# A gated-recurrence and feed-forward kernel: the last token tile's second layer in two column parts, and room for the factor DMAs in SyncE's queue

## The chip, the cores and the metric

The kernel runs on one core of one Trainium2 chip. The metric is the device time of one execution in microseconds, as the median of several timed runs. Beside them stands one profiled execution, from which all durations below are taken. Engines are named TensorE (PE in the profile), VectorE (DVE), ScalarE (ACT), GpSimd (POOL) and SyncE (SP).

## The reference

Two steps follow each other. For each of 4 batches and 8 heads, a state of 48 x 48 runs over 768 time steps:

```python
for t in range(S):
    state = alpha[:, :, t, :, None] * state + np.einsum('bhd,bhe->bhde', k[:, :, t], v[:, :, t])
    y[:, :, t] = np.einsum('bhd,bhde->bhe', q[:, :, t], state)
```

The result, with heads side by side, is x with 3072 tokens of 384 numbers. Then a feed-forward block:

```python
h = x @ w_in            # 384 -> 2048
r = np.maximum(h, 0.0)
g = r * r
return (g @ w_out).astype(np.float32)   # 2048 -> 384
```

Inputs and the output are float32.

## The kernel before

**Tiles.** The 3072 tokens are 24 chunks of 128, six for each batch. One chunk s is also one token tile of the feed-forward block. The recurrence is done in chunk form: ScalarE takes the logarithm of alpha (`L_s`, L404), TensorE sums it along the chunk with a triangular matrix (step p0), ScalarE takes exponentials of that (`A` or `Af`, L432, and `Ainv`, L436), VectorE forms `qA_s` = q x A (L462) and `kI_s` = k x Ainv (L465), TensorE transposes both (steps p1q, p1k, L256), and from there come masked scores (`sm`, L526), the state (`st`) and the chunk's output. The state is multiplied once for each chunk by the chunk's total factor (`ae_s`, L560), and a copy of it (`sb`, L565) serves the next chunk. GpSimd casts v (`vb`, L409).

**Feed-forward.** For each group of token tiles, the first layer's matmuls (`bank<-xT_big,w_in_b`) are followed by a ReLU on ScalarE (`r`, L814) and a square on VectorE (`gT`, L822); the second layer (`bank<-w_out_b,gT`) runs 16 matmuls of 384 columns for each token tile, in four quarters, into one PSUM bank. The tile's result is copied to `ob` (L852 on VectorE or L854 on ScalarE) and stored by a DMA of 192 KB from SyncE's queue (L861; L864 for the first four tiles).

**The factor.** For chunks below `TURN` = 12 the chunk's factor comes out of TensorE and ScalarE. From chunk 12 on it is the last row of `Af`, brought to the partitions of `ae_s` by two small DMAs, also from SyncE's queue (`e_aed`, L447 to L449).

**The order.** The order of all instructions on each engine is worked out before the launch by a planner (class `Plan`). Each operation has an engine, a duration and what it depends on; `run` places the operation that can start first, and at the end `self.order.sort(key=lambda o: o.start)` gives the order in which all are emitted. The planner has columns that are no engine of their own: "DMA" for the loads, first in first out; "OUT" for the stores; "SPD" for the factor DMAs. All three are emitted into the one queue of SyncE, which issues in order and waits where the next DMA has to wait. A placed store pushes the DMA column back by its duration:

```python
            if eng == "OUT":
                free["DMA"] = max(free.get("DMA", 0.0), t) + op.dur
```

A factor DMA does not. A store's `start` is moved back by `OUT_LATE` = 3.5 (attribute `late`, line 865) against the time at which it is ready, so that it is emitted behind what the planner places in these 3.5.

**Loads.** Each chunk has four loads of 192 KB, in the order at (alpha), qt, kt, vt (`add_load`, L347). The buffers hold pairs of chunks, three pairs deep (`LB` = 6 chunks). The planner lets the load of chunk s start when the use of the same tensor of chunk s-6 is done (`prev`), and counts `LD` = 1.05 for it.

**Durations in the planner** that the change meets: a quarter of the second layer 0.65; the copy of a tile on ScalarE 0.38; steps from an operation's end to its users 0.05 behind the second layer, 0.14 behind ScalarE, 0.13 behind VectorE; `Af` 0.76; `qA_s` from chunk 12 on 0.78; a store 0.55; a factor pair 0.4, landing `AE_LAT` = 4.0 later. They set orders only.

Of the kernel before, what the change touches and what calls it, by code (L numbers as in the profile page):

```python
# [8 lines left out]
FP32 = mybir.dt.float32  # L9
# [47 lines left out]
def after(op, x=0.0):  # L57
    return (op, x)


class Plan:
# [37 lines left out]
    def run(self, gate):  # L99
        free = self.free  # L100
        while any(self.pending.values()):
            best = None
            for eng, ops in self.pending.items():
                t0 = free.get(eng, 0.0)
                pick = None
                fifo = eng in ("DMA",)
                for op in (ops[:1] if fifo else ops):
                    if not gate(op):
                        continue
                    r = self.ready(op)  # L110
                    if r is None:
                        continue
                    if len(op.durs) > 1:
                        ends = {e: max(r, free.get(e, 0.0)) + x + LAT[e] for e, x in op.durs.items()}
                        if ends[eng] > min(ends.values()):
                            continue
                    key = (max(r, t0), op.prio)
                    if pick is None or key < pick[0]:
                        pick = (key, op)
                if pick is not None and (best is None or pick[0][0] < best[0]):  # L120
                    best = (pick[0][0], eng, pick[1])
            assert best is not None, "nothing can run"
            t, eng, op = best
            for e in op.durs:
                self.pending[e].remove(op)
            op.eng, op.dur = eng, op.durs[eng]
            op.start = t + getattr(op, "late", 0.0)
            if eng == "DMA" and self.pauses and t >= self.pauses[0][0]:
                op.dur += self.pauses.pop(0)[1]
            free[eng] = t + op.dur  # L130
            if op.lat is None:
                op.lat = LAT.get(eng, 0.2)
            if eng == "OUT":
                free["DMA"] = max(free.get("DMA", 0.0), t) + op.dur
            op.done = t + op.dur + op.lat
            if op.takes is not None:
                self.ready(op)
                op.slot.release.append(op.gives if op.gives is not None else op)
            self.order.append(op)
            self.on_pick(op)  # L140
        self.order.sort(key=lambda o: o.start)
# [3 lines left out]
def kernel(  # L145
# [10 lines left out]
    nc = tc.nc  # L156
    B, H, S, D = q.shape
    HD = H * D
    P = 128
# [3 lines left out]
    d_model, d_ff = moe_w_in.shape  # L163
    n_tok = out.shape[0]
    KT = d_model // P
    FT = d_ff // P
    NT = n_tok // P
# [5 lines left out]
    out_r = out.rearrange("(tt p) n -> tt p n", p=P)  # L173
# [7 lines left out]
    LB = 6  # L181
# [3 lines left out]
    opool = ctx.enter_context(tc.tile_pool(name="opool", bufs=9))  # L185
# [15 lines left out]
        out=utri_f, in_=ones_f, compare_op=ALU.is_ge, fill=0.0,  # L201
# [4 lines left out]
        out=sutri_f, in_=ones_f, compare_op=ALU.is_ge, fill=0.0,  # L206
# [25 lines left out]
    w_out_b = consts.tile([P, FT, d_model], BF16)  # L232

    NBUF = 4
    TURN = 12
# [13 lines left out]
    def pin(ins):  # L249
        tc.keep_in_program_order(ins)  # L250

    def mm(*a, **kw):
        pin(nc.tensor.matmul(*a, **kw))  # L253
# [4 lines left out]
    plan = Plan()  # L258
# [9 lines left out]
    def psum(op, shape, dt):  # L268
        i = op.slot.bank
        return banks[i].tile(shape, dt, name=f"bank{i}")  # L270
    X_SLACK = 0.2
    LD = 1.05
# [4 lines left out]
    def add(eng, dur, emit, *deps, **kw):  # L277
        return plan.add(Op(eng, dur, emit, deps, **kw))
# [42 lines left out]
    def w_dep(which, f):  # L321
        return w_ready[which][[hi > f for hi in W_CUT[which][1:]].index(True)]

    C = [dict() for _ in range(NT)]
# [13 lines left out]
    def add_load(s, nm):  # L338
        d = C[s]
        b, c = divmod(s, NCH)  # L340
        k = s // 2

        def ld():
            if s % 2 == 0:
                PAIR[k][nm] = loads.tile([P, 2, H, D], FP32, name=nm)
            d[nm] = PAIR[k][nm][:, s % 2]
            pin(nc.sync.dma_start(out=d[nm], in_=SRC[nm][b, c]))  # L347
        prev = C[s - LB]["use_" + nm] if s - LB >= 2 * NS else None
        if 2 * NS <= s < 2 * NS + LB and (k - LB // 2) < NS:
            prev = SUP[k - LB // 2]["use_" + nm]  # L350
        d["ld_" + nm] = add("DMA", LD, ld, prev, lat=2.4)

    PAIR = [dict() for _ in range(NT // 2)]
    SRC2 = [("at", alpha), ("qt", q), ("kt", k), ("vt", v)]
# [39 lines left out]
    def add_chunk(s):  # L394
        d = C[s]
# [4 lines left out]
        g = dict(prio=-10.0 + s * 0.01)  # L400
# [49 lines left out]
        if s < TURN:  # L450
            ae0 = add("ACT", 0.18, e_ae0, p0, after(ai), **g)
            p0.gives = ae1 = add("ACT", 0.19, e_ae1, p0, after(ae0), **g)
        else:
            p0.gives = ai
            ae1 = add("SPD", 0.4, e_aed, a_, lat=AE_LAT, **g)

        def e_qA():
            if s < TURN:
                pin(nc.vector.tensor_mul(qA[:, :, 0:D], d["qt"], d["A"]))
            else:  # L460
                v4 = "p (n j) d -> p n j d"
                pin(nc.vector.tensor_mul(qA[:, :, 0:D].rearrange(v4, j=2), d["qt"].rearrange(v4, j=2), d["A"]))  # L462
# [312 lines left out]
    GT = [sum(GN[:i]) for i in range(len(GN))]  # L775
    NG = len(GN)
    gT = {}
    NQ = 4
# [2 lines left out]
    M2_LAST = sl_bank[::-1]  # L781
    OUT_LATE = 3.5
    OUT_AT = 72.0
    RELU_PRIO = -20.0
    RELU_PRIO0 = 0.0
    DUMMY = 1
    COLD = 8.0
    sq = {}
    prog = {"m1": 0.0, "m2": 0.0}

    def add_moe1(g, f0, before, lo=0, hi=None, per=1):
# [20 lines left out]
        def e_relu():  # L812
            box["r"] = rpool.tile([P, 512], BF16, name="r")
            pin(nc.scalar.activation(box["r"][:, 0:w], box["ph"][:, 0:w], AF.Relu))  # L814
        rl = add("ACT", 0.055 + w / 1190.0, e_relu, op, prio=RELU_PRIO if g > 1 else RELU_PRIO0)
        box["first"].gives = rl
# [9 lines left out]
            sq.setdefault((g, f0 + i), []).append(o)  # L826
        return op

    def add_moe2(g, tt, before, box, quarters, pools):

        for qd in quarters:
            def e_mm(qd=qd):
                if qd == 0:
                    box["po"] = psum(box["first"], [P, 512], FP32)[:, 0:d_model]
                for kf in range(qd * FT // NQ, (qd + 1) * FT // NQ):
                    mm(box["po"], lhsT=gT[g][:, kf, tt * P:(tt + 1) * P], rhs=w_out_b[:, kf, :],
                       start=(kf == 0), stop=(kf == FT - 1))
            fs = range(qd * FT // NQ, (qd + 1) * FT // NQ) if g == 0 else range(FT)
            deps = [o for f in fs for o in sq[(g, f)]] + [w_dep("o", fs[-1] if g == 0 else FT - 1)] + ([after(before)] if before else [])
            op = plan.add(Op("PE", 0.65, e_mm, deps, takes=pools if qd == 0 else None, prio=0.1))  # L840
            op.moe = (2, 2.56 / NQ)
            if qd == 0:
                box["first"] = op
            op.lat = 0.05
            before = op
        if quarters[-1] < NQ - 1:
            return op

        def e_ev():
            box["ob"] = opool.tile([P, d_model], FP32, name="ob")  # L850
            if ev.eng == "DVE":
                pin(nc.vector.tensor_copy(box["ob"], box["po"]))  # L852
            else:
                pin(nc.scalar.copy(box["ob"], box["po"]))  # L854
        ev = add({"DVE": 0.47, "ACT": 0.38}, 0, e_ev, op, prio=-15.0)
        box["first"].gives = ev

        def e_out():
            s = GT[g] + tt
            if s >= 2 * NS:  # L860
                pin(nc.sync.dma_start(out=out_r[s], in_=box["ob"]))  # L861
            else:
                for t in range(2):
                    pin(nc.sync.dma_start(out=out2_r[s, t], in_=box["ob"][HF * t:HF * t + HF]))  # L864
        add("OUT", 0.55, e_out, ev, at=OUT_AT + 3.0 * (GT[g] + tt)).late = OUT_LATE
        return op

    DMA_ORDER = ["0 at qt kt vt", "1 at qt kt", "i", "1 vt", "i", "i", "i", "i", "o", "o", "o", "o"]
    for x in DMA_ORDER + [s for s in range(2 * NS, NT) if s not in DMA_ORDER]:
        if x in ("i", "o"):  # L870
            load_w(x)
        elif isinstance(x, str):
            for nm in x[1:].split():
                add_load2(int(x[0]), nm)
            if len(SUP[int(x[0])]) == len(srcs) * 1:
                add_super(int(x[0]))
        else:
            for nm, _ in srcs:
                add_load(x, nm)
            add_chunk(x)  # L880
# [84 lines left out]
```

## Time and profile before

| | |
|---|---|
| median of 3 timed runs | 187.55 us (187.5, 187.55, 188.36) |
| profiled execution | 188.04 us |
| its span | 186.3 us, 5003 instructions |
| busy share of the span: PE, DVE, ACT, POOL | 95%, 73%, 66%, 16% |
| PE matmuls | 1986 |
| DMA moved | 30.23 MB in 100712 packets, mean 162 GB/s |
| stores of a tile (L861) | 20, 192 KB each, 2.5 us median to landing |
| factor DMAs (L449) | 24, 0.8 KB each, 2.0 us median to landing |
| loads (L347) | 20 for each tensor, 192 KB each, 3.7 to 3.8 us median to landing |

The span runs from the first to the last instruction of the profiled execution, and the execution's own time is 1.7 us longer. In the profile's rows the first number is the start in microseconds from the span's start and the second the duration; "x4" counts instructions merged into one row. Rows of SPq are SyncE's issues of DMAs: their duration is that of the issue, with the time it had to wait inside, not that of the transfer. Matmul rows overlap, since the end of a matmul is modelled: the pitch of a run of matmuls is read from their starts.

### The profile page before, as it was taken

To read this page: it belongs to the slowest core of one execution; us is meant where nothing else is said; L and a number is where in the kernel's file an instruction comes from. 1 tells how busy PE (TensorE), PEld (TensorE's weight loads), DVE (VectorE), ACT (ScalarE), POOL (GpSimd) and SP (SyncE) were. 2 spreads that over 40 slices of the span, in tenths; PEclk is the share of its full clock that TensorE was granted. 3 is DMA by queue.
4 is the path that set the end of the run, shared out by engine and by line. 5 is a ranking of instruction groups with operands and counts; after the bars stand their busy time and mean duration, and the time that the engine had idled before them with its cause. 6 is when DMAs were issued, how large, how long until landed. Compare 5 with 4: busy or idle time off the path is not lost.

```text
span 186.3 us, 5003 instructions
## 1 busy us (share of the span) xinstructions
PE 177.9 (95%) x1986; PEld 132.6 (71%) x1987; DVE 136.5 (73%) x281; ACT 122.6 (66%) x257; POOL 29.8 (16%) x47
## 2 busy tenths in 40 slices
PE   7889899999999999999999999799999999999992
PEld 2566684667887877777867878467878778777751
DVE  6688679875996986776997988664997977952500
ACT  3577779457986975847758778428867847744621
POOL 5034777411111121011011012001020000000000
PEclk9999999999999999999999999999999999999999
DMA  6999999799999999892899679888101011011112
GB/s 149 261 279 344 382 372 325 153 219 214 179 183 203 188 197 202 196 205 50 186 250 201 154 173 226 162 184 191 66 0 43 4 44 44 4 42 46 42 48 81
DMA packets 100712, 30.23 MB, mean 162 GB/s; under 512 B 93648, under 2 KB 99536, under 8 KB 100688
## 3 DMA queue, kind: packets, MB, share of 16 engines
q1 hardware_dynamic: 100688, 29.91, 68.4%
q8 instruction: 15, 0.25, 0.6%
q14 instruction: 9, 0.07, 0.1%
HBM read 25.17 MB, written 4.72 MB: 160 GB/s over the span
## 4 chain that ended last, share of the span: by engine, by line
PE 81%; DMA 6%; DVE 4%; ACT 3%; SPq 3%; issue 1%; DVEq 0%; ACTq 0%
PE bank L253 70%; PE bank L256 7%; DMA at<-in_alpha_dram 3%; PE sc L253 2%; SPq L362 2%; PE st L253 2%; DMA vt<-in_v_dram 2%; DMA ae_s<-Af 1%; DVE gT L822 1%; DVE qkT L369 1%; ACT raw L713 1%; ACT r L814 1%; DVE st L560 1%; ACT A L632 0%; ACT L_s L601 0%
## 5 line engine op out<-in xcount | busy, mean ns | idle before, releaser
L253 PE MATMUL bank<-xT_big,w_in_b 128*128 128x256 bf16 (+2 forms) x599 | 73.8, 268 | 0.1
L253 PE MATMUL bank<-w_out_b,gT 128*128 128x384 bf16 x384 | 72.0, 326 | 0.0
L814 ACT ACTIVATE r<-bank 128x512 bf16<-128x512 f32 x96 | 56.6, 602 | 18.3 <-PE bank L253 16.7
L253 PEld LDWEIGHTS <-w_in_b 128*128 128x128 bf16 x600 | 52.9, 98 | 10.0
L822 DVE TENSOR_TENSOR gT<-r 128x512 bf16<-128x512 bf16 x96 | 45.1, 496 | 13.1 <-ACT r L814 12.8
L253 PEld LDWEIGHTS <-gT 128*128 128x128 bf16 x384 | 35.4, 97 | 18.2
L409 POOL CAST vb<-vt 128x384 bf16<-128x384 f32 x20 | 11.3, 566 | 93.8 <-PE bank L253 51.7
L369 DVE COPY qkT<-bank 128x1024 bf16<-128x1024 bf16 (+1 forms) x26 | 16.5, 646 | 2.9 <-PE bank L256 2.7
L854 ACT COPY ob<-bank 128x384 f32<-128x384 f32 x19 | 9.2, 483 | 14.1 <-PE bank L253 14.0
L526 DVE TENSOR_TENSOR sm<-sc,utri_b 128x512 bf16<-128x512 f32 x24 | 15.4, 682 | 2.2 <-PE sc L253 2.2
L367 ACT CAST xn<-bank 128x384 bf16<-128x384 f32 x24 | 11.2, 481 | 8.8 <-PE bank L253 8.6
L369 DVE COPY xT_big<-bank 128x384 bf16<-128x384 bf16 x21 | 7.4, 354 | 10.2 <-PE bank L256 10.1
L253 PEld LDWEIGHTS <-qkT 64*128 64x128 bf16 (+2 forms) x304 | 10.5, 97 | 5.1 <-issue 2.3
L462 DVE TENSOR_TENSOR qA_s<-qt,Af 128x384 bf16<-128x384 f32 x12 | 10.3, 860 | 3.1 <-ACT Af L432 2.9
L565 ACT CAST sb<-st 128x384 bf16<-128x384 f32 x16 | 7.7, 478 | 6.2 <-DVE st L560 6.1
L465 DVE TENSOR_TENSOR kI_s<-kt,Ainv 128x384 bf16<-128x384 f32 x20 | 11.6, 582 | 0.0
L432 ACT ACTIVATE Af<-bank 128x384 f32<-128x384 f32 x12 | 10.4, 865 | 1.2 <-ACT L_s L404 0.6
L256 PE MATMUL bank<-ident_bf,kI_s 128*128 128x128 bf16 x96 | 9.2, 220 | 1.5 <-DVE kI_s L465 1.4
L404 ACT ACTIVATE L_s<-at 128x384 bf16<-128x384 f32 x20 | 10.3, 525 | 0.4 <-DMA at<-in_alpha_dram 0.4
L253 PE MATMUL bank<-warm 128*128 128x256 bf16 (+2 forms) x39 | 8.7, 355 | 1.9 <-DVE both L216 1.1
L560 DVE TENSOR_TENSOR st<-st,ae_s 128x384 f32<-128x384 f32 x16 | 8.9, 558 | 1.9 <-DMA ae_s<-Af 1.8
L436 ACT ACTIVATE Ainv<-bank 128x384 bf16<-128x384 f32 x20 | 10.3, 514 | 0.0
(72 smaller groups left out, 176.7 us busy)
## 6 DMA issues: line engine op xcount, KB each, us to landing
at<-in_alpha_dram SPq DMA_DIRECT2D x20, 192.0 KB, 3.8
qt<-in_q_dram SPq DMA_DIRECT2D x20, 192.0 KB, 3.8
kt<-in_k_dram SPq DMA_DIRECT2D x20, 192.0 KB, 3.7
vt<-in_v_dram SPq DMA_DIRECT2D x20, 192.0 KB, 3.7
out_dram<-ob SPq DMA_DIRECT2D x20, 192.0 KB, 2.5
wo<-in_moe_w_out_dram SPq DMA_DIRECT2D x4, 768.0 KB, 6.9
wi<-in_moe_w_in_dram SPq DMA_DIRECT2D x3, 768.0 KB, 8.0
at<-in_alpha_dram SPq DMA_DIRECT2D x2, 384.0 KB, 4.9
```

Of the source, the lines that this page charges most:

```text
L253: pin(nc.tensor.matmul(*a, **kw))
L256: pin(nc.tensor.transpose(*a))
L367: pin(nc.scalar.copy(out_t, in_t))
L369: pin(nc.vector.tensor_copy(out_t, in_t))
L404: pin(nc.scalar.activation(L[:, :, 0:D], d["at"], AF.Ln))
L409: pin(nc.gpsimd.tensor_copy(d["vb"], d["vt"]))
L432: pin(nc.scalar.activation(d["A"], split(d["pm"][:, 0:HD], s), AF.Exp))
L465: pin(nc.vector.tensor_mul(kI[:, :, 0:D], d["kt"], d["Ai"]))
L526: pin(nc.vector.tensor_mul(d["sm"][:, hh], d["sc"][hh], utri_b.to_broadcast([P, NP, P])))
L560: pin(nc.vector.tensor_mul(st4, st4, bcast(ae, D)))
L814: pin(nc.scalar.activation(box["r"][:, 0:w], box["ph"][:, 0:w], AF.Relu))
L822: pin(nc.vector.tensor_mul(gT[g][:, f0:f0 + per, lo * P:lo * P + n], r, r))
```

## The change

The planner gets three new rules. A factor pair now pushes the DMA column back by 0.5 (`hold`). A load of chunk 14 or later waits in the plan also for the use of the same tensor of chunk s-5 (`pace`). A load of chunk 12 or later counts 0.97 and not 1.05. None of the three adds a wait on the chip by itself; they alter start times in the plan, and so the order of emission.

The last token tile's second layer is computed by a new function, `add_last`: first 16 matmuls for columns 0 to 255 into one bank, then 16 matmuls for columns 256 to 383 into another. Each part has its own copy, always on ScalarE, and its own store, of 128 KB and of 64 KB, without `late`.

```diff
@@ run
+            if hasattr(op, "hold"):
+                free["DMA"] = max(free.get("DMA", 0.0), t) + op.hold
             if eng == "OUT":
                 free["DMA"] = max(free.get("DMA", 0.0), t) + op.dur
@@ add_load
-        d["ld_" + nm] = add("DMA", LD, ld, prev, lat=2.4)
+        pace = C[s - LB + 1]["use_" + nm] if s >= TURN + 2 else None
+        d["ld_" + nm] = add("DMA", LD if s < TURN else 0.97, ld, prev, pace, lat=2.4)
@@ add_chunk
             ae1 = add("SPD", 0.4, e_aed, a_, lat=AE_LAT, **g)
+            ae1.hold = 0.5
@@
+    LAST_COLS = ((0, 256), (256, 384))
@@
+    def add_last(g, tt, before, pools):
+        deps = [o for f in range(FT) for o in sq[(g, f)]] + [w_dep("o", FT - 1)]
+        rows = out_r[GT[g] + tt]
+        for lo, hi in LAST_COLS:
+            box = {}
+            for qd in range(NQ):
+                def e_mm(qd=qd, lo=lo, hi=hi, box=box):
+                    if qd == 0:
+                        box["po"] = psum(box["first"], [P, 512], FP32)[:, 0:hi - lo]
+                    for kf in range(qd * FT // NQ, (qd + 1) * FT // NQ):
+                        mm(box["po"], lhsT=gT[g][:, kf, tt * P:(tt + 1) * P], rhs=w_out_b[:, kf, lo:hi],
+                           start=(kf == 0), stop=(kf == FT - 1))
+                t = 0.65 * (hi - lo) / d_model
+                op = plan.add(Op("PE", t, e_mm, deps + [after(before)], takes=pools if qd == 0 else None, prio=0.1))
+                op.moe = (2, t)
+                box.setdefault("first", op)
+                op.lat = 0.05
+                before = op
+
+            def e_ev(lo=lo, hi=hi, box=box):
+                box["ob"] = opool.tile([P, hi - lo], FP32, name=f"ob{lo}", tag="ob")
+                pin(nc.scalar.copy(box["ob"], box["po"]))
+
+            def e_out(lo=lo, hi=hi, box=box):
+                pin(nc.sync.dma_start(out=rows[:, lo:hi], in_=box["ob"]))
+            ev = add("ACT", 0.3, e_ev, op, prio=-15.0)
+            box["first"].gives = ev
+            add("OUT", 0.3, e_out, ev)
+        return op
+
     def add_moe2(g, tt, before, box, quarters, pools):
+        if GT[g] + tt == NT - 1:
+            return add_last(g, tt, before, pools)
```

## The prediction

> **What bounds the kernel now.** I read the busy table and the 40 slices first, then who waited for whom on TensorE, then the chain of waits around the one large wait, then SyncE's timeline in front of it, and last the end of the span.
>
> ```profile
> PE 177.9 (95%) x1986; PEld 132.6 (71%) x1987; DVE 136.5 (73%) x281; ACT 122.6 (66%) x257; POOL 29.8 (16%) x47
> ...
> PEclk9999999999999999999999999999999999999999
> ```
>
> TensorE is busy for 95% of the span, at full clock. So only three things can move the time: TensorE's work, its few waits, and the 3.5 us after its last matmul (182.79 to 186.29). TensorE's waits by releaser:
>
> ```profile
> PE bank L256 <- DVE kI_s L465: 1.4, 1, 1.4
> PE bank L253 <- DVE both L216: 1.1, 1, 1.1
> PE bank L253 <- ACT r L814: 0.8, 1, 0.8
> ```
>
> The second and third belong to the start. The table by stretches of time agrees: TensorE is busy for 16.00 of 84 to 100 us, 16.97 of 100 to 117, 2.62 of 117 to 121, 39.00 of 121 to 160. From 84 us on there is one hole, before the transposes of kI_s. The chain of waits goes through it:
>
> ```profile
> 116.58 2.05 DMA ae_s<-Af
> ...
> 118.82 0.57 DVE st L560
> 119.39 0.32 DVE gT L822
> 119.71 0.48 DVE kI_s L465
> ...
> 120.23 0.40 PE bank L256 x4
> ```
>
> VectorE stands at the state product (L560), which needs the factors ae_s from a DMA; behind it in VectorE's order are a square and kI_s, and TensorE waits for kI_s. Each chunk from 12 on issues one pair of factor DMAs (L449), so the pairs count off the chunks: 84.61 is chunk 12, 89.35 is 13, 100.12 is 14, 103.89 is 15, and this one is 16. Why it is late stands in SyncE's and ScalarE's timelines:
>
> ```profile
> 112.49 1.16 SPq L347 DMA_DIRECT2D at<-in_alpha_dram  x1
> 113.71 0.77 SPq L347 DMA_DIRECT2D qt<-in_q_dram  x1
> 114.52 1.26 SPq L347 DMA_DIRECT2D kt<-in_k_dram  x1
> 115.88 1.29 SPq L449 DMA_DIRECT2D ae_s<-Af  x2
> ```
> ```profile
> 110.54 0.86 ACT L432 ACTIVATE Af<-bank 128x384 f32<-128x384 f32 x1 [0.56 <-ACT L_s L404]
> ```
>
> Af of chunk 16 is ready at 111.40, its DMA issues at 115.88: for 4.5 us it stands behind loads. Counting loads in fours, these three are at, qt and kt of chunk 21, first used some 15 us or more later.
>
> **The change, part one: SyncE's order.** `hold` and `pace` alter only the planner's DMA column. They touch another engine's order only where an operation was ready last because of a load. After 84 us the trace shows no ScalarE or VectorE wait for a load, only GpSimd's vb casts, and those are far off the path (GpSimd 16% busy). So I take all compute orders as unchanged except in the last tile. What moves is the emission order on SyncE. From chunk 14 on, the load of qt of s is planned only when qA of s-5 is done, and qA takes Af, as the factor DMA does: the factor of s-5 is ready when qA starts, at least 0.91 (0.78 + 0.13 of the code's constants) before qt of s may start. The order is sorted by planned start, so qt21 and, the column being first in first out, kt21 and vt21 fall behind factor 16. at21 stays ahead of it, since its pace is the logarithm of chunk 16, before Af. Adding up the column with 0.97 per load, 0.55 per store and 0.5 per factor pair also puts one load more ahead of the pairs of chunks 12 (qt16), 13 (at17), 14 (at19) and 15 (kt19), and the last q, k, v loads of chunk 23 behind factor 18.
>
> Gain at the hole. Two loads less ahead of factor 16: 113.71 to 115.88 = 2.17 us, so its landing goes from 116.58 + 2.05 = 118.63 to 116.46. VectorE finishes the square before the product at 116.63 + 0.41 = 117.04. From there the chain as it stands, 118.82 to 120.23 = 1.41, makes the transposes ready at 118.46 (Ainv, ended at 117.61, is in time). TensorE is free at 117.38 + 8 x 0.162 = 118.68 (0.162 is the pitch of these 384-column matmuls: (7.96 - 0.33)/47 in the last run of 48). So the hole, 118.68 to 120.23 = 1.55, closes, with 0.2 us to spare on VectorE and 0.8 us on the DMA. Bounds: 1.2 if a square has to wait in between, 1.55 at most. As nothing waits on TensorE between 121 and 183, everything after moves up in full. I take -1.55.
>
> Costs elsewhere. Pairs 14 and 15 get one load more in front but also lost one: qt16 now issues at about 81.8, while SyncE stood idle for Af of chunk 12 until 84.61; after that SyncE issues without a pause to 126. The count of issues ahead of pairs 14 and 15 is therefore the same as before. Zero, covered by VectorE's 0.6 us between the landing of pair 14 (101.48 + 2.2 = 103.7) and its product at 104.29; without that cover each further microsecond costs up to one. Pair 18 waits for its Af at 127.84 with the queue empty; the loads now behind it are used after 138. Zero.
>
> **Part two: the last tile.** The code says which store goes last, and it is not the new one. Every other store is placed 3.5 (`late`) after its copy; the two new ones are placed at once. In planner constants from the end T of the second-last tile's matmuls: its store sits at T + 0.05 + 0.38 + 0.14 + 3.5 = T + 4.07; the 256-part's at T + 1.73 + 0.05 + 0.3 + 0.14 = T + 2.22, the 128-part's at T + 2.60 + 0.49 = T + 3.09. Both new stores go ahead of the 192 KB store of the tile before, though that is ready first. SyncE works in order, so this store now leaves last.
>
> The end now, from the timelines of all engines and of SyncE:
>
> ```profile
> 170.89 4.09 PE L253 MATMUL bank<-xT_big,w_in_b 128*128 128x256 bf16 x36
> ...
> 174.82 7.96 PE L253 MATMUL bank<-w_out_b,gT 128*128 128x384 bf16 x48
> ...
> 182.82 0.48 ACT L854 COPY ob<-bank 128x384 f32<-128x384 f32 x1 [2.12 <-PE bank L253]
> ```
> ```profile
> 183.32 0.33 SPq L861 DMA_DIRECT2D out_dram<-ob  x1
> ```
>
> and, for 128 columns, from TensorE's timeline earlier:
>
> ```profile
> 46.61 0.83 PE L253 MATMUL bank<-xT_big,w_in_b 128*128 128x128 bf16 x12
> 47.28 0.39 PE L256 MATMUL bank<-ident_bf,qA_s 128*128 128x128 bf16 x4
> ```
>
> On the old clock: the last tile's matmuls were 16 x 0.162 = 2.59. They become 16 x 0.109 (256 columns: (4.09 - 0.27)/35) + 16 x 0.056 (128 columns: 12 from 46.61 to 47.28) = 2.64, so +0.05, end 182.84. The 256-part's copy and store lie beside the 128-part's matmuls. No row has a 128x128 copy; 384 columns take 0.483 and 512 take 0.602, 0.93 ns per column, so 0.25 (bounds 0.17, the 64x4 row, and 0.48): it ends at 183.12, the store issues at 183.14. The store of the tile before follows: two DMAs in a row stand 0.56 apart at 127.84 (x2 in 1.14); bounds 0.38 (0.33 and a step) and 0.66 (x2 in 1.32 at 76.33). So 183.70, and 1.94 from issue to landing, as the last store has now: 185.64 against 185.26. I take +0.38, bounds +0.2 to +0.6. The own banks save nothing: no matmul waited for a copy here.
>
> The sum: -1.55 + 0.38 = -1.17. The profiled execution took 188.04 (span 186.3 and 1.7 around it), so 186.87; the three timed runs have median 187.55, so 186.38, say **186.4**. With the bounds 1.2 to 1.55 and 0.2 to 0.6: 186.2 to 186.95.
>
> The Trainium skill, TensorE: Matmul & The Clock Gate, section Back-to-back issue gap, speaks against narrow parts: it gives some 81 ns per matmul with 128 columns in a stream with weight loads, by which the 128-part would take 1.30 instead of 0.90 and the sum be 186.8. This case's pitch of 0.056, with a weight load for each matmul, is lower. Rival 5 is the mechanism, priced from rows.
>
> **Rivals.** (1) The wait reappears at an earlier pair: at19 ahead of pair 14 meets an issue as slow as that of qt at 107.78 (2.65), VectorE, full from 103 to 109, starts the product late, and TensorE, with some 0.25 us between sm and its use at 108.29, stops. Price 0 to 1.8, half of it 0.9: 187.3. For it: spare of 0.6 only. Against: the equal count above. (2) Factors are no earlier (the loads ahead are drained no faster, and the DMA lands behind at21's 4.2 us as before): only the tail is left, +0.38: 187.9. Against: SyncE reaches it two issues earlier. (3) Slower: the last store sticks behind the two others. Its place is the final landing; the store issued at 105.91 took 4.8 against 1.94, price +2.9: 186.4 + 2.9 = 189.3. It decides from a landing of 1.94 + 1.17 = 3.1 on. Against: that one had loads in front of it; the last stores land in 1.8 to 1.9, and only 192 KB precede this one. (4) The order comes out as one would wish, the 128-part last: its store lands earlier by the smaller copy and by up to 0.45 of transfer, 0.6 in all before 185.26: -1.55 - 0.6, 185.4. Against: the constants above. (5) Weight loads bind the 128-part: 16 x 0.097 = 1.55, +0.65: 187.0. Against: the 0.056 pitch.
>
> **How the numbers follow.** A measurement of this kernel can tell about 0.5%, 0.94 us, from no change: below 186.61 is faster. Forecast 0.59, two thirds of its range on the faster side; (1) 0.13, (2) 0.09, (3) 0.08, (4) 0.08, (5) 0.03. Faster 0.39 + 0.08 = 0.47; slower 0.08; within 0.45. The likeliest range is 186.2 to 186.95; the range for 8 in 10 runs from 186.0 to 188.0, taking in (1), (2) and (5), leaving out (3) and (4).
>
> **What would show it.** Right: SyncE's timeline has the pair of chunk 16 directly behind an at load and issued near 113.7; the wait of PE for kI_s is gone; the last SyncE issue is a 192 KB store some 0.5 us behind a 64 KB one; TensorE's end to span's end is about 3.9 instead of 3.5. Wrong: a VectorE wait for ae_s at another product, a TensorE wait over 0.5 us between 84 and 183, a 64 KB store as the last issue, or a last landing over 3 us.

## The result and the profile after

The changed kernel took 186.78 us (median of 10 runs, 186.55 to 187.31), the kernel before 188.11 beside it (10 runs, 187.19 to 188.95). The ratio is 0.994, 95% interval 0.9917 to 0.9964: about 1.1 us faster. (The quotient of the means is 0.994 too, that of the medians 0.993; in the experiments the ratios leave out executions in a slower state, and the medians do not.) The prediction was 186.4, with 186.0 to 188.0 as its range and -1.17 us as its sum. The profiled span is 185.5 us against 186.3. The profiled execution after is among the slower of its ten (187.25).

SyncE's timeline after, around the factor pair of chunk 16 (start, duration of the issue, engine, line):

```profile
112.68 0.75 SPq L349 DMA_DIRECT2D at<-in_alpha_dram  x1
113.52 2.24 SPq L452 DMA_DIRECT2D ae_s<-Af  x2
115.82 0.58 SPq L349 DMA_DIRECT2D qt<-in_q_dram  x1
```

The pair now stands directly behind the at load of chunk 21, and qt of 21 behind it. It starts at 113.52 (forecast 113.7; before 115.88). VectorE after:

```profile
105.32 0.57 DVE L564 TENSOR_TENSOR st<-st,ae_s 128x384 f32<-128x384 f32 x1 [0.64 <-DMA ae_s<-Af]
...
117.30 0.42 DVE L827 TENSOR_TENSOR gT<-r 128x512 bf16<-128x512 bf16 x1
117.63 0.56 DVE L564 TENSOR_TENSOR st<-st,ae_s 128x384 f32<-128x384 f32 x1
118.10 0.42 DVE L827 TENSOR_TENSOR gT<-r 128x512 bf16<-128x512 bf16 x1
118.43 0.55 DVE L469 TENSOR_TENSOR kI_s<-kt,Ainv 128x384 bf16<-128x384 f32 x1
```

At chunk 16 the state product follows the square at once, and kI_s comes 0.8 us behind it. At chunk 14 there is something new: the product at 105.32 stood 0.64 us waiting for its factors. TensorE after, at both places:

```profile
107.40 0.81 PE L255 MATMUL bank<-w_out_b,gT 128*128 128x384 bf16 x4
108.39 0.33 PE L255 MATMUL bank<-sb,qkT 128*128 128x96 bf16 x4 [0.18 <-DVE sm L530]
```
```profile
118.04 1.46 PE L255 MATMUL bank<-w_out_b,gT 128*128 128x384 bf16 x8
119.34 0.39 PE L258 MATMUL bank<-ident_bf,kI_s 128*128 128x128 bf16 x4
```

118.04 + 8 x 0.162 = 119.34: the hole of 1.55 is closed to nothing. But 107.40 + 4 x 0.162 = 108.05 against 108.39 is a new hole of 0.34, and a second one of 0.23 follows it (the next group starts at 108.99, while eight matmuls from 108.56 at 0.025 each are done at 108.76): 0.57 lost. In the kernel before the same groups stand without a gap:

```profile
107.10 0.81 PE L253 MATMUL bank<-w_out_b,gT 128*128 128x384 bf16 x4
107.75 0.33 PE L253 MATMUL bank<-sb,qkT 128*128 128x96 bf16 x4
```

107.10 + 4 x 0.162 = 107.75, and the next group starts at 108.12, just when the eight matmuls from 107.92 are done. The end after, from the timeline of all engines:

```profile
181.46 1.12 SPq L858 DMA_DIRECT2D out_dram<-ob  x2
181.96 0.27 ACT L855 COPY ob<-bank 128x128 f32<-128x128 f32 x1 [0.52 <-PE bank L255]
182.64 0.41 SPq L898 DMA_DIRECT2D out_dram<-ob  x1
```

L858 is the line of the two new stores, L898 that of the tile before: its 192 KB leave last, as forecast. From the start of the last copy to the end of the span it is 3.5 us (181.96 to 185.5), as before (182.82 to 186.3).

In the profiles, then: -1.55 at chunk 16, +0.57 at chunk 14, about +0.1 at the end (the last run of matmuls spans 8.00 against 7.96, and what follows 3.54 against 3.48), and -0.20 at a small hole of the kernel before that is gone: the transposes of qA_s at 112.90 were done at 112.90 + 4 x 0.056 = 113.12 there, those of kI_s started at 113.32, and after they follow at once (113.77 and 113.99). These make -1.1. Another +0.3 is there by chunk 12, whose pair, bound to Af, issues at 84.91 and not at 84.61. It arises in the first 20 us (TensorE is busy for 16.69 of them before and for 16.38 after), ahead of the first load that the new rules touch, that of chunk 12, issued at 61.61 in the kernel before; so the new rules do not explain it. With it the sum is -0.8, as the spans differ.

### The profile page after: what moved, and what is told of

It is laid out like the page before. It is cut to its first block, busy times and chain, and to the rows that moved or that the text cites. A ratio compares the mean times of both kernels' runs of the same rounds, so it can differ in the third digit from the quotient of the medians.

```text
span 185.5 us, 5043 instructions
## 1 busy us (share of the span) xinstructions
PE 177.8 (96%) x2003; PEld 133.8 (72%) x2003; DVE 136.2 (73%) x281; ACT 122.8 (66%) x258; POOL 29.5 (16%) x47
## 4 chain that ended last, share of the span: by engine, by line
PE 75%; DMA 8%; SPq 8%; DVE 3%; ACT 3%; issue 1%; DVEq 0%
PE bank L255 66%; PE bank L258 6%; SPq L365 4%; DMA wi<-in_moe_w_in_dram 4%; DMA out_dram<-ob 2%; PE sc L255 2%; PE st L255 1%; DMA ae_s<-Af 1%; DVE sm L530 1%; SPq L349 1%; ACT Af L435 1%; ACT r L819 1%; SPq L898 1%; SPq L300 1%; DVE st L564 1%
## 5 line engine op out<-in xcount | busy, mean ns | idle before, releaser
L255 PE MATMUL bank<-w_out_b,gT 128*128 128x384 bf16 (+2 forms) x400 | 72.1, 319 | 0.0
L827 DVE TENSOR_TENSOR gT<-r 128x512 bf16<-128x512 bf16 x96 | 44.3, 488 | 13.3 <-ACT r L819 13.0
L255 PEld LDWEIGHTS <-gT 128*128 128x128 bf16 x400 | 36.4, 98 | 17.4
L412 POOL CAST vb<-vt 128x384 bf16<-128x384 f32 x20 | 10.8, 545 | 93.0 <-PE bank L255 56.1
L891 ACT COPY ob<-bank 128x384 f32<-128x384 f32 x18 | 8.7, 484 | 11.9 <-PE bank L255 11.7
L530 DVE TENSOR_TENSOR sm<-bank,utri_b 128x512 bf16<-128x512 f32 x16 | 10.2, 679 | 0.0
L258 PE MATMUL bank<-ident_bf,qA_s 128*128 128x128 bf16 x96 | 9.3, 219 | 0.5 <-DVE qA_s L653 0.3
```

The source lines that it names most:

```text
L258: pin(nc.tensor.transpose(*a))
L412: pin(nc.gpsimd.tensor_copy(d["vb"], d["vt"]))
L530: pin(nc.vector.tensor_mul(d["sm"][:, hh], d["sc"][hh], utri_b.to_broadcast([P, NP, P])))
L827: pin(nc.vector.tensor_mul(gT[g][:, f0:f0 + per, lo * P:lo * P + n], r, r))
```

## The experiments

My theory, called the theory of place: the gain is the factor pair's earlier place in SyncE's queue, and the planner's rules matter only through that order. The rivals: the split end brings the gain, or the "room" as such does (denser loads). As a common measure, the trace's table by stretches of time gives TensorE's busy time in the 12 us from 100 to 112 and the 10 us from 112 to 122, of the one profiled execution of each kernel. It counts a matmul as busy to its modelled end, so it shows holes too small: of the 0.57 at chunk 14 above it shows 0.24.

| kernel | 100 to 112 | 112 to 122 | ratio of times to the kernel before, interval |
|---|---|---|---|
| before | 12.00 | 8.59 | 1 |
| whole change | 11.76 | 10.00 | 0.994 (0.9917 to 0.9964) |
| e1 split end alone | 12.00 | 9.49 | 1.0011 (0.9981 to 1.0041) |
| e2 three planner rules alone | 11.26 | 10.00 | 0.9915 (0.9882 to 0.9948) |
| e3 pace alone | 11.64 | 10.00 | 0.9902 (0.9867 to 0.9938) |
| e4 denser loads alone | 11.71 | 8.58 | 1.0032 (0.9995 to 1.0068) |
| e5 hold alone | 12.00 | 10.00 | 0.9925 (0.9905 to 0.9945) |

The ratios of e1 to e4 share one set of runs of the kernel before, those of e5 to e8 another, those of e9 to e12 a third, each set on another chip.

**e1, the split end alone.** Edit, against the changed kernel:

```diff
-            ae1.hold = 0.5
-        pace = C[s - LB + 1]["use_" + nm] if s >= TURN + 2 else None
+        pace = None
-        d["ld_" + nm] = add("DMA", LD if s < TURN else 0.97, ld, prev, pace, lat=2.4)
+        d["ld_" + nm] = add("DMA", LD, ld, prev, pace, lat=2.4)
```

> The last tile in two parts as changed, the planner as before. Theory of place (the gain comes from the factor pair of chunk 16 standing two loads earlier in SyncE's queue): the TensorE wait for kI_s stays (about 1.4 us), the 192 KB store still leaves last, and the time is 0.0 to 0.4 us above the kernel before. Rival theory of the end (the split brings the gain): 0.4 to 1.2 us below, with TensorE's end to the end of the span under 3.2 us.

Measured: no difference, and by the interval at most 0.4 us of gain: the split end does not bring what the whole change brought. The wait for kI_s is there, but smaller than expected:

```profile
PE bank L258 <- DVE kI_s L468: 0.5, 1, 0.5
```

Its SyncE order is that of the kernel before up to the last stores, and yet this hole is 0.5 and not 1.4: its pair issued at 114.74, 1.1 us earlier than in the kernel before, so the hole's size differs from one execution to the next. (The profiled execution is the fastest of its twelve, 187.83.) Most of what it gained there it lost at the end: 4.2 us from the start of the last copy to the end of the span (181.93 to 186.1), against 3.5 in the kernel before:

```profile
181.93 0.27 ACT L854 COPY ob<-bank 128x128 f32<-128x128 f32 x1 [0.52 <-PE bank L255]
182.90 0.33 SPq L897 DMA_DIRECT2D out_dram<-ob  x1
```

Here the last store followed the 64 KB one by 0.68 us (182.22 to 182.90) and landed 2.2 us after its issue.

**e2, the three planner rules alone.** Edit, against the changed kernel:

```diff
-        if GT[g] + tt == NT - 1:
-            return add_last(g, tt, before, pools)
```

> The planner's three rules as changed, the last tile as before. Theory of place: the wait for kI_s is gone, a wait of about 0.6 us of VectorE for the factors of chunk 14 is there with about 0.5 us lost on TensorE near 108 us, and the time is 0.8 to 1.4 us below the kernel before, no worse than the whole change. Rival theory of the end: within 0.3 us of the kernel before.

Measured: the whole gain (1.6 us by the ratio, interval 1.0 to 2.2), so the planner's rules carry it. VectorE waits 1.3 us for the factors of chunk 14 in the profiled execution, twice what was expected; at 187.83 us it is the slowest of the eight.

**e3, pace alone.** Edit: e2, and

```diff
-            ae1.hold = 0.5
-        d["ld_" + nm] = add("DMA", LD if s < TURN else 0.97, ld, prev, pace, lat=2.4)
+        d["ld_" + nm] = add("DMA", LD, ld, prev, pace, lat=2.4)
```

> Only pace: no hold, loads count 1.05, the last tile as before. In SyncE's queue nothing differs from before down to the at load of chunk 21; then the factor pair of chunk 16 comes ahead of qt and kt of chunk 21. Theory of place: the wait for kI_s is gone, no new wait at chunk 14, since its pair stands ahead of the at load of chunk 19 as before: 1.3 to 1.7 us below the kernel before, some 0.5 us better than the three rules together. Rival theory of spacing (room in the queue from denser loads and hold is what helps): within 0.4 us of the kernel before.

Measured: pace alone gives the whole gain, as expected, and the rival of spacing falls. But "no new wait at chunk 14" was wrong. SyncE's timeline of e3:

```profile
101.50 0.39 SPq L349 DMA_DIRECT2D vt<-in_v_dram  x1
101.98 1.29 SPq L452 DMA_DIRECT2D ae_s<-Af  x2
103.33 0.58 SPq L349 DMA_DIRECT2D at<-in_alpha_dram  x1
```

The order is that of the kernel before, vt of 18, pair 14, at of 19, but the pair issues at 101.98 and not at 100.12, VectorE stands idle for 0.77 us before the product at 105.39, and TensorE is busy for 11.64 of the 12 us. (The trace puts the 0.77 down to TensorE's matmuls of sc, which end last; but in the profile of the whole change the product starts while those still run, and here the pair's two DMAs land at about 105.1 and 105.3.) So at of 19 in front of the pair is not needed for this wait: with the same order down to there it was absent in the profiles of the kernel before and of e1 and present in that of e3.

**e4, denser loads alone.** Edit: e2, with `ae1.hold` removed and `pace = None`; loads from chunk 12 on still count 0.97.

> Only the denser count of loads (0.97): no hold, no pace, the last tile as before. Factor pairs now stand behind two loads more at chunks 14, 15 and 16 (14 behind qt of 19, 15 behind vt of 19, 16 behind at of 22), and qt of 16 ahead of pair 12. Theory of place: all three pairs land about 1 to 2.5 us later, the wait for kI_s grows from 1.4 to 2.5 us or more and a wait at chunk 14 appears: 1 to 4 us above the kernel before. Rival theory of spacing: 0.3 to 1.3 us below.

Measured: not faster, so the rival of spacing falls again; 0.6 us slower by the ratio, with no difference just inside the interval, which is less than expected. SyncE's timeline and VectorE's waits:

```profile
115.88 1.06 SPq L349 DMA_DIRECT2D at<-in_alpha_dram  x1
117.04 1.41 SPq L452 DMA_DIRECT2D ae_s<-Af  x2
```
```profile
DVE st L563 <- DMA ae_s<-Af: 2.5, 2, 1.8
```

The pair stands behind at of 22 and issues at 117.04; two products wait, 2.5 us together. The places came out as expected, and pair 16 is some 1.2 us later; but TensorE's work in front of the hole is 1.1 us later as well (118.44 against 117.38), 0.5 of it from before chunk 14 and the rest by the wait there, so the hole at chunk 16 stayed at 1.4.

**e5, hold alone.** Edit: e2, with `pace = None` and `LD` for all loads; `hold` stays.

> Only hold: no pace, loads count 1.05, the last tile as before. The factor pair of chunk 14 now stands one load earlier than in the kernel before, 15 two loads earlier, 16 two loads earlier, directly behind at of 21. Theory of place, carried over to chunk 14 (the wait there comes from the loads ahead of its pair): neither chunk 14 nor chunk 16 shows a VectorE wait for factors over 0.3 us, TensorE loses nothing over 0.2 us between 84 and 183, and the time is 0.3 to 0.8 us below that of pace alone, 186.0 to 186.5. Rival theory (the wait at chunk 14 is there whatever the order): 0.4 us or more lost there, and the time of pace alone, 186.6 to 187.0.

Measured: 186.8 us. Both waits are gone, as the theory had it; the time is that of pace alone and not 0.3 to 0.8 below, so this half of the expectation failed. SyncE and VectorE in e5:

```profile
99.65 0.38 SPq L349 DMA_DIRECT2D kt<-in_k_dram  x1
100.12 1.29 SPq L452 DMA_DIRECT2D ae_s<-Af  x2
```
```profile
104.51 0.56 DVE L564 TENSOR_TENSOR st<-st,ae_s 128x384 f32<-128x384 f32 x1
```

Pair 14 stands ahead of vt of 18, one place earlier than in the kernel before, and its product does not wait. The profiled execution is the fastest of its six (186.44, of 186.44 to 187.05). All four profiles with `hold` and loads counted at 1.05 (e5, e6, e7, e11) lack the wait at chunk 14; all four with `hold` and 0.97 (the whole change, e2, e8, e12) have it. How often it occurs in the runs without a profile is not known.

**e6 and e7, the end with this order.** e6 is the whole change with loads counted at 1.05; its factor pairs stand as in e5. e7 adds:

```diff
-        add("OUT", 0.55, e_out, ev, at=OUT_AT + 3.0 * (GT[g] + tt)).late = OUT_LATE
+        add("OUT", 0.55, e_out, ev, at=OUT_AT + 3.0 * (GT[g] + tt)).late = OUT_LATE if GT[g] + tt < NT - 2 else 0.0
```

> The whole change, but loads count 1.05 again: factor pairs stand as with hold alone, the last tile in two parts with the 192 KB store leaving last. Theory of place: as hold alone plus 0.0 to 0.3 us for the end (TensorE's end to the end of the span 3.5 to 3.8). Rival theory of the end (the split helps by itself): 0.2 us or more below hold alone.

> As the run before it in this list, but the store of the tile before the last is placed when it is ready, so that the 64 KB store leaves last. If the order of the stores is what takes the split's gain away: TensorE's end to the end of the span falls to 2.9 to 3.2, and the time is 0.4 to 0.6 us below that run. If not: no difference over 0.15 us.

Measured: e6 186.8 (186.61 to 186.93), ratio 0.9926 (0.9905 to 0.9946); e7 186.46 (186.13 to 186.66), ratio 0.9908 (0.9889 to 0.9927). e6 stands level with e5: the split as written gains nothing. e7 is 0.34 lower by the medians, short of 0.4 to 0.6. Its end:

```profile
181.24 1.12 SPq L858 DMA_DIRECT2D out_dram<-ob  x2
181.73 0.27 ACT L855 COPY ob<-bank 128x128 f32<-128x128 f32 x1 [0.52 <-PE bank L255]
```

No issue follows the two new stores. From the start of the last copy to the end of the span (184.8) it is 3.1 us, in e6 3.6 (181.52 to 185.1).

**e8, the whole change with the stores' order mended.** Edit: the line of e7, in the changed kernel.

> The whole change with only the order of the last stores mended (the store of the tile before the last placed when it is ready). If the order of the stores is what takes the split's gain away: 0.4 to 0.6 us below the whole change, 186.2 to 186.4, with a last issue of 64 KB. If not: 186.6 to 186.9. The wait for the factors of chunk 14 stays as in the whole change in both cases.

Measured: 186.68, ratio 0.9924 (0.9903 to 0.9946). In its profile the end falls to 2.9 (181.68 to 184.6), as expected; the median is on the side of no difference, and VectorE again waits 0.6 for the factors of chunk 14. By time alone e8 settles nothing.

**e9, the factor DMAs from ScalarE.** Edit, against the kernel before:

```diff
-                pin(nc.sync.dma_start(out=ae_s[HF * j:HF * j + D, i, j], in_=d["Af"][P - 1:P, j]))
+                pin(nc.scalar.dma_start(out=ae_s[HF * j:HF * j + D, i, j], in_=d["Af"][P - 1:P, j]))
```

> The kernel before, with the factor DMAs issued by ScalarE behind Af and not by SyncE: nothing else of the order changes. If the pair of chunk 16 is late because of its place in SyncE's queue: it issues within 0.3 us of the end of Af, lands 2 us later or less, and no wait for factors and no wait for kI_s is left, 1.3 to 1.7 us of TensorE's time. If the 16 DMA engines' backlog behind the issue is what counts: it lands 3 us or more after its issue, though still before its use. On ScalarE 24 issues of some 0.6 (as on SyncE) are new, 14 us in a row of 66% busy; where they delay Ainv or r, TensorE pays. Time 1.5 below to 0.5 above the kernel before.

Measured: ratio 1.0232 (1.0203 to 1.0262), 4.4 us slower, far outside what was expected. Around the pair of chunk 16 (ScalarE's timeline, then TensorE's waits):

```profile
112.86 0.86 ACT L432 ACTIVATE Af<-bank 128x384 f32<-128x384 f32 x1 [0.74 <-PE bank L253]
113.51 0.53 ACT L436 ACTIVATE Ainv<-bank 128x384 bf16<-128x384 f32 x1
113.75 1.15 ACTq L449 DMA_DIRECT2D ae_s<-Af  x2
114.95 0.52 ACT L404 ACTIVATE L_s<-at 128x384 bf16<-128x384 f32 x1 [0.91 <-ACT Ainv L436]
```
```profile
PE bank L253 <- ACT r L814: 3.0, 5, 1.1
```

The pair is issued within 0.1 us of Af's end, lands 2.7 to 3.0 after its issue, and no wait for factors is left. Of the wait for kI_s, 0.5 us in three pieces is left. But ScalarE starts nothing else during the 1.15 us of the two issues, and TensorE now waits for r: 3.0 us in total, against 0.8 before. The waits that the trace lists make up some 2 of the 4 us by which the span grew; the rest is not traced.

**e10, the factor DMAs from GpSimd.** Edit: e1 with the line of e7, and `nc.gpsimd.dma_start` in the place of e9's edit.

> The planner as before, the factor DMAs issued by GpSimd, the last tile in two parts with the 64 KB store last. GpSimd is 16% busy and its casts of v are far off the path, so if only the place in SyncE's queue was wrong: no wait for factors, none for kI_s, TensorE's end to the end of the span 2.9 to 3.2, and 186.0 to 186.6 us, the best of all or level with hold and the mended order. If an issue from GpSimd lands later than 4.5 us behind Af: a wait for factors is left, 187 or more.

Measured: 186.41 us (186.15 to 186.55), ratio 0.9917 (0.9892 to 0.9941). The pair of chunk 16, whose Af runs from 111.23 for 0.86:

```profile
112.39 0.99 POOL L452 DMA_DIRECT2D ae_s<-Af  x2 [2.16 <-ACT Af L435]
```

The factors leave 0.3 us behind Af with the planner of the kernel before, and no wait for them or for kI_s is left, at chunk 14 either. This is the plainest evidence for the theory of place: taking the pairs out of SyncE's queue does the same as moving them forward in it (e7, with the same end, has 0.9908).

**e11 and e12, the best version beside the whole change, on one chip.** e11 is the kernel of e7, e12 the changed kernel.

> The kernel with hold, pace, loads counted at 1.05, and the mended order of the last stores, beside the whole change on one chip: 0.2 to 0.6 us below it, by the wait at chunk 14 (0 to 0.6) and the end (0.5).

> The whole change once more, as the measure for the run before it in this list: 186.6 to 187.2, with the wait at chunk 14 and an end of 3.5 to 3.7.

Measured: e11 186.28 (186.07 to 186.44), ratio 0.9912 (0.9885 to 0.994); e12 187.05 (186.52 to 187.49), ratio 0.9951 (0.9933 to 0.9968). The slowest run of e11 is faster than the fastest of e12: 0.77 us by the medians, more than the 0.2 to 0.6 expected. In e12's profile VectorE waits 0.7 us at chunk 14 and the end is 3.6 (182.19 to 185.8); in e11's there is no such wait and the end is 3.0 (181.38 to 184.4). e11 beats both kernels.

## Why the prediction was right

**The sum**, -1.17 against about -1.1 measured, came out near in part by luck. Of the parts above, chunk 16 was forecast as it came; chunk 14 cost 0.57 where nothing was forecast, the small hole at 113 gave 0.20 that was not forecast, and the end cost about 0.1 and not 0.38. These three errors cancel to 0.1.

**The order** of SyncE's queue came out as worked out from the code at every place that was named: pair 16 behind at of 21, one load more ahead of pairs 12 to 15, the 192 KB store last.

**The hole at chunk 16**, -1.55: right in size. VectorE's part of the chain was right to 0.2 us: forecast was the square done at 117.04 and transposes ready at 118.46; in the profile after, which is some 0.7 us later by then (118.04 against 117.38), the product starts at 117.63 right behind its square. The landing, forecast for 116.46, came at about 117.1: the pair was issued in time, but its first DMA took 1.6 us to issue, so the second started at 115.2 and landed 1.9 later. Half a microsecond was left before the product. One point was too narrow: I gave the closing to pace. e3 and e5 show that pace alone and hold alone each do it.

**Zero at chunk 14** failed. The step was "The count of issues ahead of pairs 14 and 15 is therefore the same as before. Zero": it counted issues and not their durations. The pairs of chunks 12 and 13, in the kernel before and after:

```profile
84.61 1.21 SPq L449 DMA_DIRECT2D ae_s<-Af  x2
89.35 1.34 SPq L449 DMA_DIRECT2D ae_s<-Af  x2
```
```profile
84.91 2.01 SPq L452 DMA_DIRECT2D ae_s<-Af  x2
90.29 1.86 SPq L452 DMA_DIRECT2D ae_s<-Af  x2
```

The pair of 12 took 2.0 us to issue and not 1.2, the pair of 13 1.9 and not 1.3, and pair 14 started at 102.00 and not at 100.12, 1.9 later, with 0.6 to spare. This is the place of rival 1, at 0.57 of its price of 0 to 1.8; but its cause, at of 19 slow in front of the pair, is not what happened: in the profile after that load took 0.42 us to issue (101.48), and e3 has the wait without it.

Why the same order issues some 2 us later in one execution than in another stays open, but the profiles narrow it. In six of them (the kernel before, e1, e5, e6, e7, e11) SyncE had been idle for 1.7 to 3.2 us when pair 12 came; the pair took 1.21 to 1.26 to issue, and no product waited at chunk 14. In the six others with the pairs on SyncE (the whole change twice, e2, e3, e4, e8) it had been idle for 0.1 to 1.3; the pair took 1.5 to 2.6, and each has the wait. In the profile after it is the load qt of 16, forecast to issue at 81.8, that ended at 83.73 and left only 1.2; in e3, with the old order, the loads ran later and ended at 83.55, against 81.71 in the kernel before. That the shorter idle time makes the pairs slow is not shown.

**The end**, +0.38: mis-sized, about 0 to 0.1 in three profiles with this end (3.5 to 3.6 against 3.5: the whole change twice, and e6), though 0.7 in that of e1. The term was the step from the 64 KB store to the next, taken as 0.56; it was 0.39 in the three (182.25 to 182.64 in the first, the second store of the 1.12 row being 0.33 long) and 0.68 in e1. The row with an empty queue, the lower bound, was the nearer one in the three. The copy of 128 columns took 0.27 against 0.25. Rival 4's mended order was worth 0.5 to 0.6 us in the profiles (e7 against e6, e8 and e11 against the whole change) and 0.34 in the medians of e6 and e7, against the 0.98 between the forecast and rival 4.

**The 128-column pitch**: the last 64 matmuls span 8.00, so 16 of 128 columns take (8.00 - 0.22 - 32 x 0.162 - 16 x 0.109)/15 = 0.057 each. Rival 5 does not hold in this kernel. The Trainium skill (TensorE: Matmul & The Clock Gate, section Back-to-back issue gap) gives some 81 ns for 128 columns; here it is 57 ns.

## What to carry to other kernels

A short DMA that others wait for must not share an in-order queue with long loads that nobody needs for 15 us, or must be given its place there by hand: follow a wait for it back to its issue, and read what was issued between its data's readiness and that. Count how long each issue takes where it will stand, not only the number of issues: the same pair of DMAs took 1.2 us to issue in one place and up to 2.6 in another. And when a planner delays some stores for good reason, a new store without that delay overtakes them: splitting the last tile paid, by 0.34 us in the medians, only once the stores left in the order in which they were ready.

## What the runs showed of the hardware that was not expected

With one and the same order up to there, SyncE reached pair 14 at 100.12 in one execution (the kernel before) and at 101.98 in another (e3); a hole can therefore come and go between executions. A factor DMA, two issues for 0.8 KB each, held ScalarE for 1.15 us, and twelve such pairs made the kernel 4.4 us slower; from GpSimd, which has room, the same two took 0.99 us and cost nothing that was seen.
